# Two cached attentions on one core: V of the second in 4096 B rows, and pairs of its quads sharing P and PV

## The chip, the cores and the metric

The kernel runs on one core of a Trainium2 chip. The metric is the device time of one execution in microseconds (us), the median of the runs. A core has a matrix engine (PE, with its weight loads shown as PEld), a vector engine (DVE), an activation engine (ACT), a pool engine, and SP, which here only issues DMA transfers. 16 DMA engines move data between HBM and the on-chip SBUF. PE writes its results to PSUM, which has eight banks of 128 partitions x 2 KB; ACT and DVE read them there.

## The reference

Two independent attention blocks, A and B, whose outputs are set side by side. Both have 16 batches, 32 query tokens, a model width of 1024, 32 query heads of 128, and a cache of 1024 keys. A has 4 key/value heads (8 query heads share one), B has 32.

```python
q = (x @ wq).reshape(B, Sq, H, Dh).transpose(0, 2, 1, 3)
scores = jnp.einsum("bhqd,bhkd->bhqk", q, k) * (Dh ** -0.5)   # A: k, v repeated 8 times over heads
p = softmax(scores)
o = jnp.einsum("bhqk,bhkd->bhqd", p, v)
out = o.transpose(0, 2, 1, 3).reshape(B, Sq, H * Dh) @ wo
```

All inputs and outputs are bfloat16. B's K and V caches are 134.2 MB each; A's are 16.8 MB each, and so is the sum over all weight matrices wq (8.4 MB each for A and B) and likewise over wo.

## The kernel before

**Planning.** The program is first written down as a list of operations, each with an engine, the resources that it reads and writes, and an assumed duration (`DUR`, L35; `PACKET`, L48, for transfers). `list_schedule` (L223) then simulates the engines with these durations and fixes the order on each engine and on SP's DMA queue, and it hands out buffer slots (`Virt` objects; `SLOTS`, L90). The order is static: on the chip each engine runs its list and waits on semaphores. Operations on "any" engine go to ACT or DVE by the planner's choice. `LOOK`, `MODE_SWITCH`, `BANK_RESERVE` steer the choice.

**Quads.** Work is cut into 128 quads of A and 128 of B, interleaved. A quad is four heads-times-batches of 32 query rows each, so 128 rows of scores over 1024 keys. For B (`mk_quadB`, L720) a quad is two batches x two neighbouring heads; four quads make a group, 32 groups go through 8 blocks of 4 heads.

**The steps of a B quad** (`quadB_all`, L940):
- K comes in as two tiles of 512 KB (`st_dmaK`, L740), each holding two heads of one batch, 64 partitions per head and 16 keys per partition, so rows of 4096 B. There are 2 x `NKB_SLOTS` = 4 raw slots.
- DVE transposes each tile in 32x32 blocks of 4-byte elements into `KBt_sb` (`st_ktrB`, L782), which holds two quads.
- Scores (L827): 32 matmuls of 32 rows x 32 columns x 512 on eight tile positions of PE, planned as four operations of eight. They use all four row groups and all four column groups, because the two heads of a K tile lie on different row groups. The results go to two banks; there are two such score buffers.
- max on DVE (L837), exp with row sum on ACT (L850), which writes P in a permuted order.
- PT (`st_ptr`, L855): P, read as pairs of bf16 in 4-byte elements, is transposed by four f32 PE transposes into one PSUM bank and copied to SBUF (`st_pev`).
- V comes in as two tiles of 512 KB (`st_dmaV`, L752): 8 keys of one head per partition row, so rows of 2048 B. There are `NVB_SLOTS` = 3 quads of slots.
- PV (L892): 32 matmuls with 128 rows on four tile positions 32 columns wide, in four operations of eight.
- reciprocal, scaling by it (L908 on ACT, L909 on DVE), a transpose (L914) and a copy into `OTB_sb`, which the output projection (`oproj`) reads.

A's quads do the same with full 128x128 tiles; their K is transposed on PE (L776). The four banks of `ps_g` serve PT, PV, projections and shuffles; two of them are reserved for the projection kind "pj" while none of that kind is held.

**Q of B** is projected per group (`qprojB`), block-transposed by DVE (L625), and spread over the row groups by PE in four operations of four matmuls per group (`qprepB_sh`, L638), each evacuated to `QR`.

**Loads.** All transfers are issued by SP in the planned order; a load that has to wait for its slot holds back every later load of the queue.

Of the kernel before, what the change touches and what calls it, by code (L numbers as in the profile page):

```python
# [7 lines left out]
ALU = alu_op_type.AluOpType  # L8
# [8 lines left out]
NVB_SLOTS = 3  # L17
NKB_SLOTS = 2
# [8 lines left out]
PE_MODE = {"scoresB": 2, "Qshuf": 2, "PVB": 1}  # L27
MODE_SWITCH = 0.05
LOOK = 0.35
STEP_US = 3  # L30
STEP_NEAR = 0
ACT_FIRST = 0.3


DUR = {  # L35
    "scoresB": (0.216, 0.20), "scoresA": (0.216, 0.20), "PT_trA": (0.49, 0.22), "PT_trB": (0.49, 0.22), "PVA": (0.45, 0.22), "PVB": (0.112, 0.22),
    "OT_tr": (0.056, 0.22), "KTA_tr": (0.45, 0.22), "Qshuf": (0.107, 0.20), "qprojA": (0.432, 0.20), "qprojB": (0.432, 0.20),
    "oprojA": (0.432, 0.20), "oprojB": (0.432, 0.20), "xT_tr": (0.45, 0.22),
    "exp": (1.10, 0.12), "PT_ev@act": (0.466, 0.13), "norm@act": (0.25, 0.13), "OT_ev@act": (0.11, 0.13), "KTA_ev@act": (0.466, 0.13),
    "qA_ev@act": (0.47, 0.13), "qB_ev@act": (0.478, 0.13), "QR_ev@act": (0.252, 0.13), "acc0@act": (0.47, 0.13), "acc0@dve": (0.58, 0.12), "xT_ev@act": (0.90, 0.13),  # L40
# [3 lines left out]
    "qA_ev@dve": (0.58, 0.12), "qB_ev@dve": (0.58, 0.12), "xT_ev@dve": (0.60, 0.12), "o_fin@dve": (0.58, 0.12), "QR_ev@dve": (0.30, 0.12),  # L44
# [3 lines left out]
PACKET = {"kb_dma": (4096, 0.159), "wq_dma": (1024, 0.046)}  # L48
# [41 lines left out]
SLOTS = {"bank": 4, "P": 3, "PT": 3, "stat": 6, "O": 2}  # L90
BANK_RESERVE = {"pj": 2}
# [14 lines left out]
class Prog:  # L106
# [61 lines left out]
    def _needs_wait(self, op, d):  # L168
        if d.dma_key is not None:
            return True  # L170
        if d.eng != op.eng:
            return True
        return op.eng in self.SELF_SYNC
# [49 lines left out]
    def list_schedule(self, lat=0.05, look=LOOK):  # L223
# [39 lines left out]
        left = {v: len(l) for v, l in uses.items()}  # L263
        slot_free = {c: [0.0] * k for c, k in SLOTS.items()}
        held = {c: [None] * k for c, k in SLOTS.items()}

        def slot_time(i):

            t = 0.0
            for v in acq[i]:  # L270
                idle = [slot_free[v.cls][x] for x in range(SLOTS[v.cls]) if held[v.cls][x] is None]
                keep = sum(k for kind, k in BANK_RESERVE.items() if kind != v.kind and not any(h is not None and h.kind == kind for h in held["bank"])) if v.cls == "bank" else 0
                if len(idle) <= keep:
                    return None
                t = max(t, sorted(idle)[0])
            return t
# [34 lines left out]
        while True:  # L311
            best = None
            bkey = None
            for eng, lst in ready.items():
# [10 lines left out]
                at = {}  # L325
                for i in lst:
                    s_ = slot_time(i) if acq[i] else 0.0
                    if s_ is not None:
                        at[i] = max(ready_t[i], fe, s_) + sw(i)
# [36 lines left out]
            for u in users[best]:  # L366
                uo = ops[u]
                same_pe = (op.dma_key is None and beng == uo.eng and uo.eng == "pe")
# [62 lines left out]
def build(nc, pa, pb, out):  # L431
# [34 lines left out]
    with stack:  # L466
# [7 lines left out]
        zeros = sb("zeros", [P, P], BF)  # L474
        id32 = sb("id32", [P, P], F32)
        z32 = sb("z32", [P, P], F32)
# [4 lines left out]
        Qtok = sb("Qtok", [P, 2, NG, CW], BF)  # L481
# [7 lines left out]
        KB_sb = sb("KB_sb", [P, 2 * NKB, 16 * Dh], BF)  # L489
        KBt_sb = sb("KBt_sb", [P, 2, 2, 16 * Dh], BF)  # L490
        VB_sb = sb("VB_sb", [P, NVB, 2, 2, NCH, Dh], BF)
# [3 lines left out]
        P_sb = sb("P_sb", [P, SLOTS["P"], Sk], BF)  # L495
        PT_sb = sb("PT_sb", [P, SLOTS["PT"], NCH, P], BF)
# [11 lines left out]
        if HOOK is not None:  # L508
            print("sbuf bytes remaining per partition:", nc.sbuf_bytes_remaining() if callable(nc.sbuf_bytes_remaining) else nc.sbuf_bytes_remaining)

        pr.add("pool", lambda g: g.memset(zeros[:], 0.0), writes=["zeros"], name="c0")
        pr.add("pool", lambda g: g.affine_select(ident[:], zeros[:], [[1, P]], ALU.not_equal, 1.0, base=0, channel_multiplier=-1),
               reads=["zeros"], writes=["ident"], name="c1")
        pr.add("pool", lambda g: g.memset(z32[:], 0.0), writes=["z32"], name="c0")
        pr.add("pool", lambda g: g.affine_select(id32[:], z32[:], [[1, P]], ALU.not_equal, 1.0, base=0, channel_multiplier=-1),
               reads=["z32"], writes=["id32"], name="c1")
# [90 lines left out]
        def qprojB(m_, G):  # L607
# [4 lines left out]
            for j0 in range(0, DJ, JS):  # L612
                def e_qp(e, j0=j0):
# [5 lines left out]
                pr.add("pe", e_qp, reads=[("wq", 1, k_) for k_ in pcs] + [("xT", 1, G)], writes=[v], claims=[("Qtok", m_ % 2, G)], name="qprojB", dur=0.225 * JS,  # L619
                       rtag=dict((("wq", 1, k_), m_) for k_ in pcs))  # L620
            evac(Qtok[:, m_ % 2, G, :], lambda: bank(v)[:, 0:CW], reads=[], writes=[v, ("Qtok", m_ % 2, G)], name="qB_ev",
                 wtag={("Qtok", m_ % 2, G): m_}, mul=scale)

        def qprepB_tr(m_, G):
            pr.add("dve", lambda e: e.transpose(QBt[:, :].bitcast(F32), Qtok[:, m_ % 2, G, :].bitcast(F32)),  # L625
                   reads=[("Qtok", m_ % 2, G)], writes=["QBt"], name="QBt_tr", rtag={("Qtok", m_ % 2, G): m_}, wtag={"QBt": (m_, G)})

        def qprepB_sh(m_, G, a_list):
            gp = (m_ * NG + G) % 2
            for a in a_list:  # L630
                v = Virt("bank", "pj")

                def e_sh(e, a=a, v=v):
                    last = None
                    for rg in range(4):
                        e_ = rg // 2
                        rhs = QBt[32 * a:32 * a + 32, :].rearrange("p (hp e x) -> p e hp x", hp=2, e=2)[:, e_, :, :]
                        last = e.matmul(bank(v)[32 * rg:32 * rg + 32, 0:2 * Dh].rearrange("p (hp x) -> p hp x", hp=2),  # L638
                                        ident[32 * a:32 * a + 32, 32 * a:32 * a + 32], rhs, start=True, stop=True,
                                        tile_position=(32 * a, 32 * rg))  # L640
                    return last
                pr.add("pe", e_sh, reads=["QBt", "ident"], writes=[v], claims=[("QR", gp, a)], name="Qshuf", rtag={"QBt": (m_, G)})
                evac(QR[:, gp, a, :, :], lambda v=v: bank(v)[:, 0:2 * Dh].rearrange("p (hp x) -> p hp x", hp=2), reads=[],
                     writes=[v, ("QR", gp, a)], name="QR_ev", wtag={("QR", gp, a): (m_, G)})
# [75 lines left out]
        def mk_quadB(t):  # L720
# [7 lines left out]
            q.hp = jb % 2  # L728
            q.b0 = 4 * q.G + 2 * q.bp
            q.h0 = q.m * MS + 2 * q.hp  # L730
            q.kvslot = t % 2
            q.krslot = t % NKB
            q.vslot = t % NVB
# [3 lines left out]
            q.kid = ("B", t)  # L737
            return q

        def st_dmaK(q, t_=None):  # L740
            if q.pi == 0:
# [5 lines left out]
            else:  # L747
                sl = (2 * q.t + t_) % (2 * NKB)
                ksrc = pb["k"][q.b0 + t_, q.h0:q.h0 + 2].rearrange("hh (p s) d -> (hh p) (s d)", s=16)
                pr.add("sp", lambda e: e.dma_start(KB_sb[:, sl, :], ksrc), writes=[("KB", sl)], dma_key=f"kb{sl}", name="kb_dma", dur=2 * Sk * Dh * 2, wtag={("KB", sl): q.kid})  # L750

        def st_dmaV(q):  # L752
            if q.pi == 0:
# [5 lines left out]
            else:  # L759
                sl = q.vslot  # L760
                for t_ in range(2):
                    vsrc = pb["v"][q.b0 + t_, q.h0:q.h0 + 2].rearrange("hh (p c) d -> p hh c d", c=NCH)
                    pr.add("sp", lambda e, t_=t_, vsrc=vsrc: e.dma_start(VB_sb[:, sl, t_, :, :, :], vsrc), writes=[("VB", sl, t_)],
                           dma_key=f"vb{sl}_{t_}", name="vb_dma", dur=2 * Sk * Dh * 2, wtag={("VB", sl, t_): q.kid})
# [17 lines left out]
        def st_ktrB(q, t_):  # L782
            sl = q.kvslot
            rs = (2 * q.t + t_) % (2 * NKB)
            pr.add("dve", lambda e: e.transpose(KBt_sb[:, sl, t_, :].bitcast(F32), KB_sb[:, rs, :].bitcast(F32)),  # L785
                   reads=[("KB", rs)], writes=[("KBt", sl, t_)], name="KBt_tr", rtag={("KB", rs): q.kid}, wtag={("KBt", sl, t_): q.kid})
# [8 lines left out]
        def st_scores(q):  # L795
            q.vS = SBuf(s_rr[0] % 2)
            s_rr[0] += 1
            q.vP, q.vPT, q.vst, q.vO = Virt("P"), Virt("PT"), Virt("stat"), Virt("O")
            q.vbt, q.vbo = Virt("bank"), Virt("bank")
# [10 lines left out]
            else:  # L810
                sl = q.kvslot
                gp = (q.m * NG + q.G) % 2

                def e_s(e, fp):
                    last = None
                    if True:
                        f, pd = fp // 2, fp % 2
                        o0 = f * 64 + pd
                        for t_ in range(2):
                            a = 2 * q.bp + t_  # L820
                            for hh in range(2):
                                cg = 2 * t_ + hh
                                for g2 in range(2):
                                    rg = 2 * hh + g2
                                    lhsT = QR[32 * rg:32 * rg + 32, gp, a, q.hp, o0:o0 + 63:2]
                                    rhs = KBt_sb[32 * rg:32 * rg + 32, sl, t_, :].rearrange("p (s x) -> p s x", s=16)[:, :, o0:o0 + 63:2]
                                    last = e.matmul(ps_s[32 * cg:32 * cg + 32, vS.idx, g2, :].rearrange("p (s j) -> p s j", s=16), lhsT, rhs,  # L827
# [297 lines left out]
```

## Time and profile before

| | |
|---|---|
| runs (us) | 901.42, 905.68, 903.89; median 903.89 |
| profiled execution: span | 902.6 us |
| TensorE clock, mean granted | 0.985 |
| moved by DMA | 341.67 MB, mean 379 GB/s |
| loads of B's V | 256 of 512 KB, 8.1 us from issue to landing (median) |
| loads of B's K | 256 of 512 KB, 9.2 us |
| K transposes on DVE (L785) | 256 of 1231 ns, 311.8 us; idle before them for DMA 40.4 us |
| max (L837), exp (L850) | 256 of 1209 ns, 256 of 1119 ns |
| PT on PE (L862) | 1024 matmuls, 177.0 us |
| B's scores (L827) | 4096 matmuls, 157.2 us |
| B's PV (L892) | 4096 matmuls, 91.1 us |

Busy time of PE is the union of its matmuls, each counted with its modelled pipeline tail, so consecutive ones overlap. A group's mean is the duration of one instruction. "From issue to landing" includes the time that a transfer queues behind earlier ones. A share of the DMA engines can pass 100%, since packets of one engine overlap a little.

### The profile page before, as it was taken

Reading aid. Unit: us, or ns where it says so; the run is one execution under the profiler, and the core shown is the slowest. Engines: PE = TensorE matmul, PEld = TensorE weight load, DVE = VectorE, ACT = ScalarE, POOL = GpSimd, SP = SyncE. Lnnn points to the kernel's source line nnn. Section 1 sums busy time; section 2 is a strip of 40 time slices with the busy share of each in tenths; the row PEclk is TensorE's granted clock in tenths of the full one; section 3 lists DMA queues with packets and bytes.
Section 4 is the critical chain, followed back from the end, with each engine's and each line's share of the span. In section 5 each row is a group of like instructions: output and inputs, shape, how many; then the busy total and the mean of one; then the engine's idle time right before and its main releaser. Section 6 shows DMA issues by size and latency. Waiting matters only on the chain.

```text
span 902.6 us, 29455 instructions
## 1 busy us (share of the span) xinstructions
PE 836.3 (93%) x12864; PEld 481.8 (53%) x12864; DVE 745.3 (83%) x1057; ACT 610.8 (68%) x1384; POOL 1.1 (0%) x8
## 2 busy tenths in 40 slices
PE   6999999999899999999999998999998988999886
PEld 4365555555555555555545455555555554555453
DVE  0578897888887999689887899878979788798885
ACT  3477886677666776676776466776867666586763
POOL 0000000000000000000000000000000000000000
PEclk9999999999999999999999999999999999999999
DMA  9999999999999999999999999999999999999994
GB/s 325 383 389 393 386 385 392 390 393 383 392 387 389 393 380 388 380 386 376 387 385 391 394 369 389 388 393 370 388 387 391 392 391 367 344 393 393 393 377 170
DMA packets 153984, 341.67 MB, mean 379 GB/s; under 512 B 12544, under 2 KB 28928, under 8 KB 153856
## 3 DMA queue, kind: packets, MB, share of 16 engines
q1 hardware_dynamic: 153856, 339.79, 100.6%
q8 instruction: 102, 1.67, 0.8%
q14 instruction: 26, 0.21, 0.1%
HBM read 337.64 MB, written 2.10 MB: 376 GB/s over the span
## 4 chain that ended last, share of the span: by engine, by line
PE 48%; DMA 23%; DVE 19%; ACT 8%; SPq 1%; issue 1%; ACTq 0%; DVEq 0%
DMA KB_sb<-in_B_k_cache_dram 21%; PE ps_s L827 10%; PE ps_g L862 9%; DVE stat L837 8%; DVE KBt_sb L785 8%; PE ps_g L680 6%; ACT P_sb L850 5%; PE ps_g L892 4%; PE ps_g L598 4%; PE ps_g L884 4%; PE ps_g L616 3%; PE ps_s L806 3%; PE ps_g L776 2%; ACT PT_sb L526 1%; PE ps_g L914 1%
## 5 line engine op out<-in xcount | busy, mean ns | idle before, releaser
L785 DVE STREAM_TRANSPOSE KBt_sb<-KB_sb 128x1024 f32<-128x1024 f32 x256 | 311.8, 1231 | 42.5 <-DMA KB_sb<-in_B_k_cache_dram 40.4
L837 DVE TENSOR_REDUCE stat<-ps_s 128x1 f32<-128x1024 f32 x256 | 304.7, 1209 | 50.7 <-PE ps_s L827 34.3
L850 ACT ACTIVATE P_sb<-ps_s,stat 128x1024 bf16<-128x1024 f32 x256 | 285.8, 1119 | 51.5 <-DVE stat L837 50.0
L862 PE MATMUL ps_g<-id,P_sb 128*128 128x128 f32 x1024 | 177.0, 300 | 13.0 <-ACT P_sb L850 4.7
L862 PEld LDWEIGHTS ps_g<-id,P_sb 128*128 128x128 f32 x1024 | 150.5, 207 | 54.9 <-issue 11.1
L827 PE MATMUL ps_s<-KBt_sb,QR 32*32 32x512 bf16 x4096 | 157.2, 399 | 19.5 <-ACT P_sb L850 10.9
L526 ACT COPY PT_sb<-ps_g 128x512 f32<-128x512 f32 x234 | 134.9, 591 | 59.5 <-PE ps_g L862 58.3
L908 ACT ACTIVATE O_sb<-ps_g,stat 128x128 bf16<-128x128 f32 x199 | 71.4, 370 | 63.0 <-PE ps_g L892 32.4
L806 PE MATMUL ps_s<-KTA_sb,QT_sb 128*128 128x512 bf16 x256 | 91.5, 388 | 6.0 <-ACT P_sb L850 5.6
L827 PEld LDWEIGHTS ps_s<-KBt_sb,QR 32*32 32x32 bf16 x4096 | 49.3, 90 | 81.1 <-ACT P_sb L850 17.8
L892 PE MATMUL ps_g<-VB_sb,PT_sb 128*32 128x128 bf16 x4096 | 91.1, 224 | 1.4 <-ACT PT_sb L526 0.9
L892 PEld LDWEIGHTS ps_g<-VB_sb,PT_sb 128*32 128x32 bf16 x4096 | 60.2, 97 | 48.7 <-issue 29.2
L884 PE MATMUL ps_g<-VA_sb,PT_sb 128*128 128x128 bf16 x1024 | 78.8, 220 | 1.8 <-ACT PT_sb L526 0.7
L884 PEld LDWEIGHTS ps_g<-VA_sb,PT_sb 128*128 128x128 bf16 x1024 | 61.6, 98 | 28.2 <-issue 8.5
L616 PE MATMUL ps_g<-wq_sb,xT_sb 128*128 128x512 bf16 x256 | 71.4, 386 | 2.9 <-DMA wq_sb<-in_B_wq_dram 2.8
L680 PE MATMUL ps_g<-woB_sb,OTB_sb 128*128 128x512 bf16 x256 | 68.7, 381 | 4.4 <-ACT OTB_sb L526 1.8
L598 PE MATMUL ps_g<-xT_sb,wq_sb 128*128 128x512 bf16 x256 | 72.0, 385 | 0.3
L680 PE MATMUL ps_g<-woA_sb,OTA_sb 128*128 128x512 bf16 x256 | 63.0, 380 | 1.3 <-DVE OTA_sb L526 1.0
L914 PE MATMUL ps_g<-ident,O_sb 128*128 128x128 bf16 x256 | 51.8, 224 | 3.0 <-ACT O_sb L908 2.0
L850 ACT ACTIVATION_READ_ACCUMULATOR P_sb<-ps_s,stat 128x1 f32 x256 | 51.8, 202 | 0.0
L526 ACT COPY OTA_sb<-ps_g 128x64 f32<-128x64 f32 x114 | 24.7, 216 | 36.7 <-PE ps_g L914 36.1
L691 DVE TENSOR_TENSOR acc<-acc,ps_g 128x512 f32<-128x512 f32 x64 | 41.2, 675 | 8.1 <-PE ps_g L680 7.6
(41 smaller groups left out, 537.5 us busy)
## 6 DMA issues: line engine op xcount, KB each, us to landing
VB_sb<-in_B_v_cache_dram SPq DMA_DIRECT2D x256, 512.0 KB, 8.1
KB_sb<-in_B_k_cache_dram SPq DMA_DIRECT2D x256, 512.0 KB, 9.2
KA_sb<-in_A_k_cache_dram SPq DMA_DIRECT2D x64, 256.0 KB, 7.7
VA_sb<-in_A_v_cache_dram SPq DMA_DIRECT2D x64, 256.0 KB, 8.1
wq_sb<-in_B_wq_dram SPq DMA_DIRECT2D x32, 256.0 KB, 8.6
wq_sb<-in_A_wq_dram SPq DMA_DIRECT2D x32, 256.0 KB, 8.8
woB_sb<-in_B_wo_dram SPq DMA_DIRECT2D x32, 256.0 KB, 9.2
woA_sb<-in_A_wo_dram SPq DMA_DIRECT2D x32, 256.0 KB, 9.1
```

The source lines that it names most:

```text
L526: return e.copy(dst, src) if hasattr(e, "activation") else e.tensor_copy(dst, src)
L598: last = e.matmul(bank(v)[:, 0:tn], wq_sb[:, 0, j, hc * Dh:(hc + 1) * Dh], xT_sb[:, 0, j, t0:t0 + tn], start=(j == 0), stop=(j == DJ - 1))
L616: last = e.matmul(bank(v)[:, 0:CW], xT_sb[:, 1, j, G * P:(G + 1) * P], wq_sb[:, 1, j, :], start=(j == 0), stop=(j == DJ - 1))
L680: last = e.matmul(bank(v)[:, 0:OUTW], OT[:, gp, hh, :], wo_[:, hh, oh * OUTW:(oh + 1) * OUTW], start=(hh == 0), stop=(hh == nh - 1))
L785: pr.add("dve", lambda e: e.transpose(KBt_sb[:, sl, t_, :].bitcast(F32), KB_sb[:, rs, :].bitcast(F32)), reads=[("KB", rs)], writes=[("KBt" ...
L806: pr.add("pe", lambda e, u=u: e.matmul(ps_s[:, vS.idx, u, :], qt[:, q.b, q.hh0:q.hh0 + 4, :].rearrange("p a q -> p (a q)"), KTA_sb[:, sl, ...
L827: last = e.matmul(ps_s[32 * cg:32 * cg + 32, vS.idx, g2, :].rearrange("p (s j) -> p s j", s=16), lhsT, rhs, start=(fp == 0), stop=(fp == 3 ...
L837: pr.add("dve", lambda e: e.tensor_reduce(stat[:, vst.idx, 0:1], ps_s[:, vS.idx, :, :], AXIS.XY, ALU.max, negate=True), writes=vS.res + [v ...
L850: return e.activation(dst, src, ACTF.Exp, bias=stat[:, vst.idx, 0:1], scale=1.0, accum_out=stat[:, vst.idx, 1:2])
L862: last = e.transpose(bank(vb)[:, m * P:(m + 1) * P], p32[:, m:Sk // 2:NPK], id32[:])
L884: last = e.matmul(bank(vb)[:, 0:Dh], ptc_of(vPT, c, 0, P), VA_sb[:, kvs, c, :], start=(c == 0), stop=(c == NCH - 1))
L892: last = e.matmul(bank(vb)[32 * a:32 * a + 32, 0:Dh], ptc_of(vPT, c, 32 * a, 32 * a + 32), VB_sb[:, kvs, a // 2, a % 2, c, :], start=(c == ...
```

## The change

Two B quads now form a pair over two batches and four heads: the quad e = 0 takes the even heads (0 and 2 of the block) and e = 1 the odd ones. A K tile still holds two neighbouring heads of one batch, so each quad of a pair uses one half (64 partitions) of all four K tiles. K is transposed in place; there are 8 K slots and no `KBt_sb`. V is loaded in the same layout as K, 16 keys per partition, in rows of 4096 B and 6 slots of one tile. The exp of both quads write one P buffer of 2048 columns, interleaved so that a 128-column block of it has 64 keys of the even head and 64 of the odd one, in V's order. PT is now eight bf16 transposes per 1024 columns, and A's P is no longer permuted. PV of a pair runs as two operations of 64 matmuls, each of 64 rows x 32 columns, on eight tile positions: the upper and lower halves of the rows belong to the two quads and write to two banks. Scores are planned as one operation of 32 matmuls, which use two row groups per quad. Q's shuffle becomes two operations of eight matmuls per group, with two evacuations of a whole bank. K loads are issued after the odd quad's scores, V loads after the pair's PV. Slot counts and planner constants change; `BOOK` holds back operations that would take a bank while one that needs two banks waits for them.

```diff
-NVB_SLOTS = 3
-NKB_SLOTS = 2
+NVB_SLOTS = 6
+NQT = 5
+NKB_SLOTS = 8
...
-MODE_SWITCH = 0.05
-LOOK = 0.35
+MODE_SWITCH = 0.1
+LOOK = 0.15
...
-SLOTS = {"bank": 4, "P": 3, "PT": 3, "stat": 6, "O": 2}
-BANK_RESERVE = {"pj": 2}
+SLOTS = {"bank": 4, "P": 1, "P2": 2, "PT": 4, "stat": 8, "O": 3}
+BANK_RESERVE = {"pj": 1}
...
+                book = max((bl[i] for i in lst if pairs[i] and ready_t[i] <= fe + BOOK and slot_time(i) is None), default=None) if eng == "pe" else None
                 for i in lst:
+                    if book is not None and acq[i] and bl[i] < book and any(v.cls == "bank" for v in acq[i]):
+                        continue
...
-        KB_sb = sb("KB_sb", [P, 2 * NKB, 16 * Dh], BF)
-        KBt_sb = sb("KBt_sb", [P, 2, 2, 16 * Dh], BF)
-        VB_sb = sb("VB_sb", [P, NVB, 2, 2, NCH, Dh], BF)
+        KB_sb = sb("KB_sb", [P, NKB, 16 * Dh], BF)
+        VB_sb = sb("VB_sb", [P, NVB, 16, Dh], BF)
...
+            for name, aa in (("Qshuf", (0, 2)), ("Qshuf2", (1, 3))):
+                pr.add("pe", lambda e, aa=aa: e_sh(e, aa), reads=["QBt", "ident"], writes=vv, claims=[("QR", gp, a) for a in aa], name=name,
+                       rtag={"QBt": (m_, G)})
...
-                for t_ in range(2):
-                    vsrc = pb["v"][q.b0 + t_, q.h0:q.h0 + 2].rearrange("hh (p c) d -> p hh c d", c=NCH)
...
+                vsrc = pb["v"][qn.b0 + x // 2, qn.m * MS + 2 * (x % 2):qn.m * MS + 2 * (x % 2) + 2].rearrange("hh (p c) d -> (hh p) (c d)", c=16)
...
-            pr.add("dve", lambda e: e.transpose(KBt_sb[:, sl, t_, :].bitcast(F32), KB_sb[:, rs, :].bitcast(F32)),
+            pr.add("dve", lambda e: e.transpose(KB_sb[:, sl, :].bitcast(F32), KB_sb[:, sl, :].bitcast(F32)),
...
+                    for fp in range(4):
+                        o0 = (fp // 2) * 64 + fp % 2
+                        for cg in range(4):
+                            t_, i = cg // 2, cg % 2
+                            for g2 in range(2):
+                                r0 = 32 * (2 * q.e + g2)
+                                lhsT = QR[r0:r0 + 32, gp, 2 * q.bp + t_, i, o0:o0 + 63:2]
+                                rhs = KB_sb[r0:r0 + 32, q.ks[cg], :].rearrange("p (s x) -> p s x", s=16)[:, :, o0:o0 + 63:2]
+                                last = e.matmul(ps_s[32 * cg:32 * cg + 32, vS.idx, g2, :].rearrange("p (s j) -> p s j", s=16), lhsT, rhs,
+                                                start=(fp == 0), stop=(fp == 3), tile_position=(r0, 32 * cg))
...
+                    src = ps_s[:, vS.idx, :, :].rearrange("p g (s j) -> p g s j", s=16)
+                    dst = P2_sb[:, vP.idx, :].rearrange("p (s e g j) -> p e g s j", s=16, e=2, g=2)[:, q.e, :, :, :]
...
+        def pt_block(name, src_of, vP, vPT, vb):
             def e_pt(e):
                 last = None
+                for c in range(NCH):
+                    last = e.transpose(bankb(vb)[:, c * P:(c + 1) * P], src_of(c), ident[:])
                 return last
...
+        def st_pvB(q0, q1):
...
+            for h in range(2):
+                pt_block("PT_trB", lambda c, h=h: P2_sb[:, vP.idx, (NCH * h + c) * P:(NCH * h + c + 1) * P], vP, vPTs[h], Virt("bank"))
...
+                    for c in range(NCH):
+                        for cg in range(4):
+                            for e_ in range(2):
+                                last = e.matmul(bank(vbs[e_])[32 * cg:32 * cg + 32, 0:Dh], PT_sb[64 * e_:64 * e_ + 64, vPTs[h].idx, c, 32 * cg:32 * cg + 32],
+                                                VB_sb[64 * e_:64 * e_ + 64, q1.vs[cg], NCH * h + c, :], start=(h == 0 and c == 0), stop=(h == 1 and c == NCH - 1),
+                                                tile_position=(64 * e_, 32 * cg))
...
+        def quadB_all(q):
+            n = q.pn
+            if q.e == 0:
+                if n == 0:
+                    for x in range(4, NKB):
+                        st_dmaK(None, x)
+                for x in range(4):
+                    st_ktrB(q, x)
+            st_scores(q)
+            if q.e == 1:
+                for x in range(4 * n + NKB, min(4 * n + NKB + 4, 2 * NIT)):
+                    st_dmaK(None, x)
+            st_max(q)
+            st_exp(q)
+            if q.e == 1:
+                q0 = quadsB[q.t - 1]
+                st_pvB(q0, q)
+                for x in range(4 * n + NVB, min(4 * n + NVB + 4, 2 * NIT)):
+                    st_dmaV(None, x)
+                finish(q0)
+                finish(q)
```

## The prediction

> **What bounds the kernel now.** I read the page from the top: busy shares, the DMA rows, the chain that ended last. Then came the DMA view of short stretches, the waits of SP's queue, and the timeline of PE for the price of single operations.
>
> ```profile
> span 902.6 us, 29455 instructions
> ...
> PE 836.3 (93%) x12864; PEld 481.8 (53%) x12864; DVE 745.3 (83%) x1057; ACT 610.8 (68%) x1384; POOL 1.1 (0%) x8
> ...
> q1 hardware_dynamic: 153856, 339.79, 100.6%
> q8 instruction: 102, 1.67, 0.8%
> ...
> PE 48%; DMA 23%; DVE 19%; ACT 8%; SPq 1%; issue 1%; ACTq 0%; DVEq 0%
> ```
>
> PE at 93% is not the bound that it seems: its matmuls are counted with their pipeline tails. The packets of q1 fill 100.6% of the sixteen DMA engines' span, so the DMA has no time left. The chain names PE most because a load starts only when an engine frees its buffer, while the data queue behind other loads: a load of K lands 9.2 us and one of V 8.1 us after its issue (medians), though 512 KB are moved in about 1.3 us.
>
> How much is lost? Cutting the span into stretches of 20 us, the best ones move 393 to 396 GB/s, and the 43 stretches from 20 to 880 us average 385.5. So 860 x (1 - 385.5/393) = 16 us of DMA time are lost to moments without work for it. The rest is rate.
>
> The rate depends on the rows. The next fence holds two stretches of 4 us: in the first nearly all loads have rows of 2 KB, in the second of 4 KB (K).
>
> ```profile
> DMA packets 833, 1.56 MB, mean 390 GB/s; under 512 B 75, under 2 KB 75, under 8 KB 832
> ...
> q1 hardware_dynamic: 832, 1.55, 104.7%
> ...
> DMA packets 467, 1.63 MB, mean 407 GB/s; under 512 B 50, under 2 KB 50, under 8 KB 467
> ...
> q1 hardware_dynamic: 467, 1.63, 103.8%
> ```
>
> Without the small packets (semaphores) these are 1.56 MB / 758 = 2058 B and 1.63 MB / 417 = 3909 B a packet. Both stretches are full (share over 103%), yet one moves 390 and the other 407 GB/s. Neighbouring cuts give 388 (from 385 to 389 us) and 410 (404.2 to 407.6), so I use 389 and 408.
>
> **The change, part by part.**
>
> V in 4 KB rows. All 256 loads of V, 134.2 MB, go from 2 KB to 4 KB packets: 134.2/0.389 = 345.0 us become 134.2/0.408 = 328.9. That is **-16 us** on the full resource. The bounds are 0 (V's source strides cancel it) and -17.7 (410 GB/s). The semaphore packets do not change, as there are 256 loads of V before and after, each still 512 KB.
>
> The Trainium skill speaks against this part: its page "DMA: Bandwidth & Descriptors", section Specifications, gives 512 B as the smallest transfer that reaches the line rate, so rows of 2 KB would already be there. By it this term would be 0. The two stretches above, 390 against 407 GB/s, do not agree with it.
>
> Instruction fetch. PT goes from 4 transposes of f32 per quad to 8 of bf16 (1024 to 2048 matmuls), and PV from 32 matmuls of 128 rows per quad to 64 of 64 rows (4096 to 8192). With a weight load each that is 2 x (1024 + 4096) = 10240 more instructions at 64 B (1.88 MB of q8 and q14 for 29455 instructions): 0.66 MB. q8's 1.67 MB took 0.8% of 902.6 = 7.2 us, so **+2.8 us** (bounds 0, if it only fills DMA gaps, and 2.8).
>
> PE. This timeline has the prices (start, duration, operation, count):
>
> ```profile
> 404.64 1.13 PE L827 MATMUL ps_s<-KBt_sb,QR 32*32 32x512 bf16 x32
> ...
> 46.66 0.63 PE L862 MATMUL ps_g<-id,P_sb 128*128 128x128 f32 x4
> 47.22 0.43 PE L827 MATMUL ps_s<-KBt_sb,QR 32*32 32x512 bf16 x8
> ...
> 48.58 0.63 PE L892 MATMUL ps_g<-VB_sb,PT_sb 128*32 128x128 bf16 x32
> 49.14 0.43 PE L827 MATMUL ps_s<-KBt_sb,QR 32*32 32x512 bf16 x8
> 49.50 0.62 PE L884 MATMUL ps_g<-VA_sb,PT_sb 128*128 128x128 bf16 x8
> ```
>
> From start to next start the four f32 transposes hold PE 0.56 us (46.66 to 47.22). Eight matmuls of 128x128 bf16 hold it 0.46 (49.50 to 49.96, the next start): 256 x -0.10 = -26 us. PV's 32 matmuls on four tiles hold 0.56 (48.58 to 49.14), one round of four per 0.06. On eight tiles a quad's 64 are eight rounds again. If a round of eight runs as one of four, +0; if PE takes the same 14 ns per matmul, 64 x 0.0144 + 0.1 = 1.02, or +0.46 x 128 = +59. The scores' eight tiles in 0.43 (L827 x8: one matmul lasts 0.40, so eight start within 0.03) are nearest, since those are also eight tiles; I take +15. Scores keep eight tiles per round, with two row groups where there were four. The bound above is rounds of four, 8 x 0.23 against 4 x 0.23, +0.9 x 128 = +118. The bound below is the gain from no longer being cut in four, 1.44 to 1.07 us (x8 holds 0.36, x32 1.07), at 57 fewer pieces (185 in the timeline now, 128 then) x 0.12 = -7; I take -7. The nearest row for one row group feeding several tiles is the shuffle (L638), whose four matmuls of 256 columns on one row group end in 0.29 us, no longer than one alone (0.28). Q's shuffle: 128 operations at 0.22 become 64 of about 0.25, -12 us. PE's sum is **-30 us** by my values, between -45 and +139 (-26 + 59 + 118 - 12). All of it lies beside the DMA, so I put it at 0 in the sum. Without that cover the chain would feel PE's part of it, 48%: -14 us by my values, +67 at the worst end, which I count under (b) below.
>
> ACT and DVE. The evacuation of Q's shuffle goes from 128 of about 0.39 us to 64 of about 0.6, -12 us. Exp, max (1.21 us), PT's evacuation (0.59) and the transposes of K (1.23, now in place) keep shape and count. All of it is hidden: DVE is busy 83% of the time. 0 in the sum, at most -12.
>
> Buffers and queue order. K held two quads raw and two transposed; now eight tiles hold two pairs. After the odd quad's scores SP issues four K loads, after the pair's PV four V loads. Behind SP's waits stand the loads of A's K and V and of the weights. Timing by pairs: 902.6/64 = 14.1 us a pair. A burst of four K loads lands 9.2 to 9.2 + 3 x 1.3 = 13.1 us after issue, and its four transposes end by 14.4, against some 20 us until the next-but-one pair's even scores. Of the V burst, the first two tiles are for the next pair, landing at 8.1 and 9.4 us against 14 until its PV. So both have 4 us or more to spare: 0, bounded by -16 (all lost DMA time comes back) and by the rival below.
>
> Start and end. The first loads keep their order, weights and x ahead of K and V. The end stays about 14 us behind the last loads (DMA share 0.07 from 890 to 902.6), because V's last two tiles come only after the last PV but one: 0, between -3 and +5 (a V load took at least 4.3 us to land).
>
> Sum: 902.6 - 16 + 2.8 = 889.4 us of span. The median of the runs, 903.89, stands 1.3 above the profiled span, so **890.7 us**, which is 1.5% less.
>
> **Rivals.**
> (a) V's rows change nothing: 903.9 + 2.8 = 906.7. For it speaks only that V's 2 KB packets may share a limit with K's that a short stretch hides; against it, the two full stretches.
> This is also what the Trainium skill's 512 B (same page and section) would give.
> (b) Slower: the pair's PV holds too much. A V slot is freed by fours, only after both halves of PV, and in that time the pair holds two PV banks and two PT banks of the four, so A's PV and the projections wait, and with them the scores that free K. Place: SP's wait before V. The present waits there are already the largest:
>
> ```profile
> SPq L763 <- PE ps_g L892: 136.7, 69, 7.4
> SPq L750 <- DVE KBt_sb L785: 115.2, 77, 5.2
> ```
>
> It decides once the queue runs dry more than (16 - 2.8)/64 = 0.21 us longer per pair than now. At 0.7 us per pair the price is 64 x 0.7 = 45 us: 890.7 + 45 - 16 (of the present loss, which it swallows) = 920. Against it: nobody waits for V in the trace, and 4 us are to spare.
> (c) Better: K's deeper slots and the lighter PE also fill the DMA's gaps, 890.7 - 14 = 877. For it: DVE still waits 40.4 us for K, and the gap stretches (319 GB/s from 318 to 322 us) follow late buffer releases; against it, the coarser bursts.
>
> **How the numbers follow.** Forecast 0.56 (its own range 881 to 899), (a) 0.10, (b) 0.22, (c) 0.12. This measurement cannot tell less than about 0.5% (899.4 to 908.4) from no change. Faster is the forecast without its slow edge plus (c), 0.66; same is (a) and that edge, 0.12; slower is (b), 0.22. The range leaves out about half of (b), above 917, and the far end of (c), below 871.
>
> **What would show it.** Right: under 121,500 packets on q1 for the same bytes, best stretches of 400 GB/s or more, q1's share still near 100%, PE's groups for PT and the shuffle smaller, no wait of PE on V. PV on eight tiles is right if 64 matmuls end in 0.7 us, wrong at 1.1; the scores are right at 1.1 us for 32. Rival (a) shows as full stretches at 390 GB/s; (b) as a q1 share well under 100% with longer waits of SP before V; (c) as an average close to the best stretches. The prediction falls if PE waits for V or for K, or if the DMA is no longer full.

## The result and the profile after

The changed kernel takes 1039.86 us (median of 4 runs, 1029.7 to 1049.9) against 904.75 us before; the ratio is 1.146, with a 95% interval from 1.140 to 1.152. The ratio leaves out the run of 1049.9 us, which fell in a slower state. It is 15% slower, where 1.5% faster was forecast, and far outside the range.

The head of the page after, its DMA rows and the shares of the chain that ended last:

```profile
span 1036.8 us, 39415 instructions
...
PE 840.4 (81%) x17829; PEld 507.8 (49%) x17984; DVE 736.0 (71%) x1014; ACT 608.5 (59%) x1363; POOL 0.7 (0%) x6
...
PEclk9989999889887988999988989989899999888987
...
q1 hardware_dynamic: 121088, 339.79, 88.1%
q8 instruction: 141, 2.31, 0.8%
...
PE 63%; issue 15%; DVE 12%; ACT 7%; DMA 2%; SPq 1%
```

No engine has noticeably more work than before: PE is busy 840 us (836 before), DVE 736 (745), ACT 609 (611). The DMA is no longer full, 88.1% after 100.6%, and the chain hardly waits for it, 2% after 23%. What is new is "issue" with 15% of the span, 155 us, where it had 1%: time in which an engine waits for nothing that the profile shows. 155 us is more than the whole loss of 134 us. PE's granted clock fell as well, from 0.985 to 0.904 on average.

The waits, longest in total first (engine, operation, what it waited for: us in total, times, longest), show which engine that is. After:

```profile
PEld ps_g L903 <- issue: 96.5, 68, 4.7
...
PE ps_g L903 <- issue: 74.9, 32, 4.6
...
PEld ps_s L839 <- issue: 44.0, 62, 3.6
```

The row of PV's weight loads before, the largest of its kind:

```profile
PEld ps_g L892 <- issue: 29.2, 72, 0.5
```

Before, "issue" was short pauses: 72 at PV, of 0.5 us at most, and none above 0.8 us in any row of the weight loads. Now PE stands still for up to 4.7 us with nothing to wait for. PE's timeline shows one such place (start, duration, operation, count, idle time before):

```profile
509.49 1.13 PE L839 MATMUL ps_s<-KB_sb,QR 32*32 32x512 bf16 x32
510.56 1.30 PE L903 MATMUL ps_g<-VB_sb,PT_sb 64*32 64x128 bf16 x128
511.79 0.62 PE L869 MATMUL ps_g<-ident,P_sb 128*128 128x128 bf16 x8
512.32 0.23 PE L925 MATMUL ps_g<-ident,O_sb 128*128 128x128 bf16 x1
513.22 0.42 PE L839 MATMUL ps_s<-KB_sb,QR 32*32 32x512 bf16 x7 [0.67 <-ACT P_sb L862]
515.77 1.07 PE L839 MATMUL ps_s<-KB_sb,QR 32*32 32x512 bf16 x25 [2.13 <-issue]
...
517.50 3.35 PE L688 MATMUL ps_g<-woB_sb,OTB_sb 128*128 128x512 bf16 x8
```

The scores of one quad are a single operation of 32 matmuls, and they stop after 7 of them: their waits were over, since seven had run. A bare lack of instructions remains. Just before, PV sent 128 matmuls with 128 weight loads through PE in 1.30 us. And 2 us behind the stop the eight matmuls of the projection take 3.35 us, 0.42 each; in the kernel before four of them took 1.03 us, 0.26 each:

```profile
417.55 1.03 PE L680 MATMUL ps_g<-woB_sb,OTB_sb 128*128 128x512 bf16 x4
```

The same place after the change by stretches, with the granted clock behind the busy times:

```profile
505.00:513.00 8.00, 7.29 (x234) 4.96 (x228) 6.97 (x14) 6.72 (x14) 0.00 (x0) 1.00 1.05 407
513.00:516.00 3.00, 0.65 (x15) 0.25 (x23) 1.84 (x2) 1.01 (x5) 0.00 (x0) 1.00 1.03 397
516.00:518.00 2.00, 2.00 (x36) 1.17 (x21) 1.12 (x1) 0.47 (x2) 0.00 (x0) 0.76 1.04 418
518.00:520.50 2.50, 2.50 (x8) 0.87 (x7) 2.50 (x4) 1.32 (x3) 0.00 (x0) 0.51 1.03 415
```

The columns are PE, PEld, DVE, ACT, POOL, clock, DMA share, GB/s. After the pause the clock is down to 0.51 for 2.5 us, so the work behind the pause is slow as well. The last two columns show the rows of 4 KB at work: full stretches (share 1.03 to 1.05) at 397 to 418 GB/s.

**Where the pauses lie.** I took all idle times of 0.9 us or more in the timeline of the weight loads that end on "issue", and counted PE's instructions (matmuls and weight loads) from one to the next:

```
at us    idle us  PE instructions since the last one
497.87   1.65      508
515.77   2.45      748
530.02   3.60      508
548.11   4.71      506
563.52   1.04      508
581.83   0.98      750
596.00   2.94      504
610.97   3.35      506
```

There are 52 such pauses, 142.7 us in sum; before there were none. Nearly all lie at a multiple of about 254 PE instructions from the one before. The queue q8 counts the same way: the change added 10,240 PE instructions and 39 packets, 263 to a packet, and a packet carries 16 KB (2.31 MB / 141). So PE gets its program in blocks of about 256.

That a pause is a block that has not come can be seen in the packets of q8 one by one, which the trace holds with their times. Of the 52 pauses, 51 end 1.2 to 1.6 us after a packet of q8 has ended, though such a packet comes only every 7 us or so; 36 of these packets started only after PE had stopped. At each pause the number of instructions that PE had run (twice its weight loads) is 186 plus 253.7 for every packet landed so far, to within 22. The pause that ends at 515.77 us began at 513.32, and its packet lies in the window from 513.5 to 514.5 us:

```profile
q8 instruction: 1, 0.02, 5.9%
```

5.9% of sixteen engines over 1 us is 0.94 us. The median packet took 0.95 us, against 1.09 us in the kernel before, so the transfer of a block is not slow: it starts too late.

The Trainium skill has this on its page "Runtime: NRT & Kernel Launch", section "Instruction fetch mechanics": blocks of 16 KiB, 256 instructions, the next fetched while the current one runs. The trace agrees with the block. The same section calls the cost of crossing a block's edge mostly hidden, and here 52 of 141 edges cost 2.7 us each.

### The profile page after: what moved, and what is told of

Same layout as the page of the kernel before. It is cut to its first block, busy times and chain, and to the rows that moved or that the text cites. A ratio compares the mean times of both kernels' runs of the same rounds, so it can differ in the third digit from the quotient of the medians.

```text
span 1036.8 us, 39415 instructions
## 1 busy us (share of the span) xinstructions
PE 840.4 (81%) x17829; PEld 507.8 (49%) x17984; DVE 736.0 (71%) x1014; ACT 608.5 (59%) x1363; POOL 0.7 (0%) x6
## 2 busy tenths in 40 slices
DMA packets 121254, 342.30 MB, mean 330 GB/s; under 512 B 12544, under 2 KB 28928, under 8 KB 121088
## 3 DMA queue, kind: packets, MB, share of 16 engines
q1 hardware_dynamic: 121088, 339.79, 88.1%
q8 instruction: 141, 2.31, 0.8%
## 4 chain that ended last, share of the span: by engine, by line
PE 63%; issue 15%; DVE 12%; ACT 7%; DMA 2%; SPq 1%
PE ps_s L839 13%; PE ps_g L688 11%; PE ps_g L869 10%; PE ps_g L903 6%; DVE stat L849 6%; PE ps_g L884 5%; PE ps_g L601 5%; PE ps_g L619 4%; ACT P_sb L862 4%; DVE KB_sb L795 4%; PE ps_s L822 4%; PE ps_g L925 2%; PE ps_g L787 2%; ACT PT_sb L529 1%; DMA VB_sb<-in_B_v_cache_dram 1%
## 5 line engine op out<-in xcount | busy, mean ns | idle before, releaser
L795 DVE STREAM_TRANSPOSE KB_sb<-KB_sb 128x1024 f32<-128x1024 f32 x256 | 308.3, 1223 | 6.3 <-DMA KB_sb<-in_B_k_cache_dram 6.0
L839 PE MATMUL ps_s<-KB_sb,QR 32*32 32x512 bf16 x4096 | 162.4, 421 | 34.5 <-issue 25.3
L869 PE MATMUL ps_g<-ident,P_sb 128*128 128x128 bf16 x2048 | 159.4, 229 | 18.1 <-issue 7.1
L869 PEld LDWEIGHTS ps_g<-ident,P_sb 128*128 128x128 bf16 x2048 | 134.7, 103 | 63.1 <-issue 15.2
L903 PE MATMUL ps_g<-VB_sb,PT_sb 64*32 64x128 bf16 x8192 | 92.7, 227 | 77.0 <-issue 74.9
L903 PEld LDWEIGHTS ps_g<-VB_sb,PT_sb 64*32 64x32 bf16 x8192 | 77.8, 91 | 105.1 <-issue 96.5
L884 PE MATMUL ps_g<-VA_sb,PT_sb 128*128 128x128 bf16 x1024 | 88.1, 236 | 14.6 <-issue 13.3
L839 PEld LDWEIGHTS ps_s<-KB_sb,QR 32*32 32x32 bf16 x4096 | 52.5, 93 | 96.5 <-issue 44.0
L822 PE MATMUL ps_s<-KTA_sb,QT_sb 128*128 128x512 bf16 x179 | 66.1, 409 | 12.4 <-issue 6.3
L529 ACT COPY OTB_sb<-ps_g 128x64 f32<-128x64 f32 x113 | 20.2, 216 | 66.0 <-PE ps_g L925 65.6
```

What stands on the lines that cost most here:

```text
L529: return e.copy(dst, src) if hasattr(e, "activation") else e.tensor_copy(dst, src)
L795: pr.add("dve", lambda e: e.transpose(KB_sb[:, sl, :].bitcast(F32), KB_sb[:, sl, :].bitcast(F32)), writes=[("KB", sl)], name="KBt_tr", rta ...
L822: pr.add("pe", lambda e, u=u: e.matmul(ps_s[:, vS.idx, u, :], qt[:, q.b, q.hh0:q.hh0 + 4, :].rearrange("p a q -> p (a q)"), KTA_sb[:, sl, ...
L869: last = e.transpose(bankb(vb)[:, c * P:(c + 1) * P], src_of(c), ident[:])
L884: last = e.matmul(bank(vb)[:, 0:Dh], PT_sb[:, vPT.idx, c, :], VA_sb[:, kvs, c, :], start=(c == 0), stop=(c == NCH - 1))
L903: last = e.matmul(bank(vbs[e_])[32 * cg:32 * cg + 32, 0:Dh], PT_sb[64 * e_:64 * e_ + 64, vPTs[h].idx, c, 32 * cg:32 * cg + 32], VB_sb[64 * ...
```

## The experiments

Theory **F**: PE's instructions are the bound. The change raised them from 25,728 to 35,968 and put 256 of them into 1.3 us; the next blocks come too late. The rival **R** is the prediction's rival (b): pairs, buffers freed by fours and the bank shortage hold things up.

**e1: more instructions, nothing else of the change.**

```diff
-  last = e.matmul(bank(vb)[32 * a:32 * a + 32, 0:Dh], ..., VB_sb[:, kvs, a // 2, a % 2, c, :],
+  last = e.matmul(bank(vb)[32 * a:32 * a + 32, x0:x0 + 64], ..., VB_sb[:, kvs, a // 2, a % 2, c, x0:x0 + 64],
...
+  for x0, c0 in ((0, 0), (0, 4), (64, 0), (64, 4)):
```

> Kernel before; each of PV's 4096 matmuls of 128 columns is cut into two of 64, with a weight load each: 8192 more PE instructions, same buffers, loads and results. Theory F (PE's instructions arrive in blocks of 256 and the block is late when PE runs through one faster than the next comes): stalls of PE on issue of 1 us and more appear, 930 to 1040 us. Theory R (pairs, freed by fours, and the bank shortage cost the time): nothing of that is in here, 900 to 912 us.

Measured: 952.96 us, ratio 1.055 (1.051 to 1.059). The kernel before, given 8192 more instructions on PE, loses 49 us; 24 long pauses of 42.6 us in sum appear, 8 of them at PV:

```profile
PEld ps_g L892 <- issue: 45.7, 85, 2.9
```

F as expected. R has no part in this kernel. Not all of the 49 us need be pauses: PE's busy time rose as well, from 836.3 to 857.1 us.

**e2: the change with half of PV's instructions.**

```diff
-                    for c in range(NCH):
+                    for c in (0, 2, 4, NCH - 1):
```

> Changed kernel; B's PV leaves out every second key chunk: 4096 matmuls and 8192 PE instructions less, pairs, banks, slots, loads and their order as in the changed kernel. F: long issue stalls of PE almost gone, 880 to 915 us. R: PV's own time was only 93 us and mostly beside other work, so above 1010 us.

Measured: 876.77 us, ratio 0.971 (0.968 to 0.974). All of the pair scheme is in it, and it is 163 us faster than the change. The page's rows for instructions and the chain:

```profile
q8 instruction: 110, 1.80, 0.7%
...
PE 41%; DVE 28%; DMA 17%; ACT 10%; issue 3%; SPq 1%; DVEq 0%
```

SP's wait before V, in the view of the waits of e2:

```profile
SPq L774 <- PE ps_g L903: 124.7, 41, 7.1
```

PE's busy time fell by only 840.4 - 770.8 = 70 us, and 9 long pauses of 15.6 us are left. R can hardly be the cause: banks, slots by fours and late V loads are all still there, though PV holds its banks for a shorter time. In the changed kernel the same wait of SP before V was 227.6 us in 55 times; it grows with PE's pauses, with the same pairs and slots in both kernels.

**e3: the rows of V alone.**

```diff
-  vsrc = pb["v"][...].rearrange("hh (p c) d -> p hh c d", c=NCH)
+  vsrc = pb["v"][...].rearrange("hh (p c) d -> (hh p) (c d)", c=2 * NCH)
```

> Kernel before; V is loaded in rows of 4096 B into the same slots, so PV multiplies V's rows in another order. No instruction more. If the row size has the worth that the prediction gave it: -16 us, 884 to 893 us. If the row size is worth nothing (rival a): 901 to 908 us.

Measured: 892.7 us, ratio 0.989 (0.985 to 0.992), 11 us faster than before. The row size is worth something, and rival (a) is out. It is worth less than the 16 us of the sum; by the chain, which hardly waits for the DMA any more (3% after 23%), PE takes over once the DMA is quicker.

```profile
PE 66%; DVE 18%; ACT 10%; DMA 3%; issue 1%; SPq 1%; DVEq 0%; ACTq 0%
```

**e4: PV in two bursts.** The second half of PT reads a token that the first half of PV writes.

```diff
+ pt_block("PT_trB", ..., ["PVhalf"])
- pr.add("pe", e_pv, reads=[vPTs[h]] + vt, writes=vbs, ...
+ pr.add("pe", e_pv, reads=[vPTs[h]] + vt, writes=vbs + ["PVhalf"], ...
```

> Changed kernel; the second half of a pair's PT is made to follow the first half of its PV, so that PV runs as two bursts of 64 matmuls with other PE work between, not as one of 128. Same instruction count. F, if the burst is what outruns the block: fewer or shorter issue stalls, 920 to 1000 us. F, if the mean rate of instructions is: about 1030 us. R: the PV banks are held longer, so not faster, 1030 us or more.

Measured: 984.91 us, ratio 1.091 (1.086 to 1.095): 55 us less than the change with exactly its instructions. Still 52 long pauses, but of 102.5 us. The burst matters beside the count. The two banks of a pair's PV are in use for longer than in the change, 4.4 us against 1.7 us in median from its first weight load to its last, and still the kernel is faster. By R it would not have been faster, so with all instructions in place R fails again.

**e5: is the block late because the DMA is full?**

```diff
+                if vt >= NVB:
+                    pr.vtag[("VB", sl)] = ("B", n, x)
+                    return
```

> Changed kernel; of B's V only the first six tiles are loaded, PV goes on reading them: 250 loads of 512 KB left out, all instructions of PE as in the changed kernel. Theory F1 (a block of instructions comes late because its transfer queues behind the data): with 40% less data the long issue stalls shrink to under 60 us in sum, below 930 us. F2 (the fetch is as slow by itself): 110 to 150 us of such stalls stay, 980 us or more.

Measured: 947.95 us, ratio 1.051 (1.048 to 1.054), 38 long pauses of 84.1 us, with q1 at 61.7% of the engines' span. That lies between both expectations. Less data traffic takes away some 40% of the pauses; more than half of them stay with the DMA idle a third of the time. All 38 end 1.2 to 1.7 us after a packet of q8, and the median packet took 0.95 us as in the change, so here too the block started late and was not slow.

**e6: eight blocks fewer.** P transposed as f32 pairs.

```diff
-                    last = e.transpose(bankb(vb)[:, c * P:(c + 1) * P], src_of(c), ident[:])
+                    last = e.transpose(bank(vb)[:, m * P:(m + 1) * P], src_of(m), id32[:])
```

> Changed kernel; P is transposed as pairs of bf16 in f32, as in the kernel before: 1024 transposes for 2048, 2048 PE instructions less of 35968, eight blocks of 141. F: fewer blocks, so a little faster, 990 to 1025 us. R: transposes are not on the path of buffers and banks, 1030 us or more.

Measured: 1018.41 us, ratio 1.128 (1.126 to 1.129), 45 pauses of 123.2 us. A little faster, as F has it.

**e7 and e8: an order that knows the blocks.** In the planner an operation of PE starts no earlier than its block is there:

```diff
+        def fetch(i):
+            return fetched[(n_pe[0] + PE_INSTR[ops[i].name] - 1) // BLOCK]
...
+                        fetched[b_ + 1] = max(st, fetched[b_]) + BLOCK_US
```

> As e6, and the planner knows that a block of 256 PE instructions can be entered only 5.5 us after the one before it was entered, so that it spreads the dense operations; LOOK 0.2, MODE_SWITCH 0.05, PV's duration 0.6. F: long issue stalls under 40 us, 870 to 920 us, so perhaps faster than the kernel before. R: 1010 us or more.

> Changed kernel with all its 35968 PE instructions; only the order is new: the planner knows the 5.5 us per block (MODE_SWITCH 0.05, ACT_FIRST 0.1, PV's duration 0.6). F: long issue stalls under 70 us, 890 to 950 us. R, or a fetch that is too slow on average: above 1000 us.

Measured: e7 1023.92 us, ratio 1.134 (1.128 to 1.139), 45 pauses of 114.3 us; e8 1016.18 us, ratio 1.126 (1.123 to 1.129), 41 pauses of 100.4 us. Both miss what F expected of them. The packets of q8 show that this says little against F. Over the whole run they came 3.3 to 14.4 us apart in e8 (the middle 80% of them 4.0 to 10.6 us), where the change had 3.3 to 15.6 us (3.6 to 11.1 us): the spacing that was planned hardly arose on the chip. It was most even from 480 to 620 us, 4.5 to 8.25 us in e8 where the change had 3.5 to 12.75, and there e8 has six pauses of 10.5 us in sum, the change nine of 23.8 us. That fits F. Whether 5.5 us is the right price of a block, and how late a block may be asked for, stays open.

**e9: the change's instruction count in the kernel before.** e1, and P in eight bf16 transposes.

```diff
-                    last = e.transpose(bank(vb)[:, m * P:(m + 1) * P], p32[:, m:Sk // 2:NPK], id32[:])
+                    last = e.transpose(bankb(vb)[:, c * P:(c + 1) * P], P_sb[:, vP.idx, c:Sk:NCH], ident[:])
```

> Kernel before with PV cut as in e1 and P transposed in eight bf16 transposes per quad: 35968 PE instructions, as many as the changed kernel, but quad by quad with the buffers and loads of before. F by count alone: as slow as the changed kernel, 1010 to 1050 us. F by count and burst (a pair's PV is 256 instructions in 1.3 us, a quad's here 128 in 0.6): 960 to 1005 us. R: 900 to 912 us.

Measured: 978.11 us, ratio 1.078 (1.072 to 1.083), 30 pauses of 60.7 us. Without pairs, with the old buffers and loads, the added instructions cost 75 us of the change's 135. By count alone it would have been as slow as the change, so the count is not all. That the rest goes with its burst is not shown by this run; e4, with the burst cut in two, gains 55 us.

**e10: halfway.**

```diff
-                    for c in range(NCH):
+                    for c in (0, 1, 2, 4, 5, NCH - 1):
```

> Changed kernel; B's PV leaves out two of eight key chunks: 4096 PE instructions less, halfway between the changed kernel and e2. F: the time lies between 877 and 1040, 930 to 985 us, and the long issue stalls between 16 and 143 us. R: above 1010 us.

Measured: 945.91 us, ratio 1.046 (1.040 to 1.052), 37 pauses of 84.9 us: between e2 and the change in time and in pauses.

**e11: both repairs.** The edits of e4 and e6 together.

> Changed kernel with both repairs, PV in two bursts as in e4 and P transposed in f32 as in e6; nothing left out. F: the gains of e4 (55 us) and e6 (20 us) add, 950 to 985 us; still above the kernel before. R: 1030 us or more.

Measured: 960.88 us, ratio 1.065 (1.062 to 1.069), 35 pauses of 73.5 us. The gains add (55 + 21 expected, 79 found), and it is the best complete version of the pair scheme that I found. It does not reach the kernel before.

All kernels in one table. The last column takes the chain's share of issue off the span.

| | PE instructions | q8 blocks | long pauses, us | issue in the chain | span, us | span less issue |
|---|---|---|---|---|---|---|
| before | 25,728 | 102 | 0 | 1% | 902.6 | 894 |
| e3 | 25,728 | 102 | 1 | 1% | 892.2 | 883 |
| e2 | 27,776 | 110 | 16 | 3% | 875.7 | 849 |
| e10 | 31,872 | 126 | 85 | 10% | 944.5 | 850 |
| e1 | 33,920 | 133 | 43 | 5% | 957.0 | 909 |
| e11 | 33,920 | 133 | 73 | 8% | 960.9 | 884 |
| e6 | 33,920 | 133 | 123 | 12% | 1021.7 | 899 |
| e7 | 33,920 | 134 | 114 | 12% | 1015.6 | 894 |
| e9 | 35,968 | 142 | 61 | 9% | 980.5 | 892 |
| e5 | 35,968 | 141 | 84 | 11% | 945.9 | 842 |
| e4 | 35,968 | 141 | 102 | 10% | 979.1 | 881 |
| e8 | 35,968 | 141 | 100 | 11% | 1019.1 | 907 |
| after | 35,968 | 141 | 143 | 15% | 1036.8 | 881 |

The spans differ by 161 us, the last column by 67 (by 60 without e5, which loads less), with no order by instruction count left in it. That ties the loss to issue, as closely as shares in whole per cent (5 us each way) can. e2, e5 and e10 also leave out work or loads.

## Why the prediction was wrong

**The step that failed** is "Instruction fetch", priced at +2.8 us. The count of 10,240 more instructions and the 0.66 MB were right, and q8 shows 39 packets more. But I priced only what these packets take from the data on the DMA, not what PE loses while it waits for one. By the chain its cost was some 146 us ("issue": 15% of 1036.8 less 1% of 902.6). With it fell the sentence that all of PE's terms lie beside the DMA: PE's work indeed did not grow, its supply ran dry.

**PE's operations** came out as priced or better. 128 matmuls of PV on eight tiles end in 1.30 us, 0.65 per half, and hold PE 1.23 us to the next start (510.56 to 511.79), 0.61 per quad against 0.56 before: some +7 us, between the lower bound of 0 and the +15 that I took. The scores with two row groups stay at 1.13 us. Q's shuffle fell from 41.0 to 20.9 us. PT's group fell from 177.0 to 159.4, less than the 26 us of the sum, though with PE's clock at 0.904. This speed is part of the trouble: the faster the tiles run, the sooner a block is used up.

**V's rows** were right in kind. q1 needs 121,088 packets, full stretches move 397 to 418 GB/s, and e3 gains 11 us, where the sum had 16 (bounds 0 and 17.7). The doubt that the Trainium skill's 512 B raised ("DMA: Bandwidth & Descriptors", Specifications) does not hold here. In the changed kernel this gain is hidden, since the DMA waits.

**Rival (b)** had the right sign and the wrong mechanism. The sign to look for, a q1 share well under 100% with longer waits of SP before V, came exactly so, yet e2 has the same pairs, banks and slots at 877 us, and e4 holds the banks longer and gains 55. The sign could not tell the two causes apart. **Rival (c)**, the better case at 877 us, is where e2 ends up, but by chance: e2 leaves out some 42 us of PE's time in PV (92.7 to 50.3) and still has 15.6 us of long pauses. What the scheme would take with its instructions in time, no run shows.

**Unsettled**: how much of the loss is the halved clock after a pause; no run here had pauses without it. Also why a block's transfer starts as late as it does, why the planned spacing of e7 and e8 hardly arose, and why e8, with pauses of 100 us, is 31 us slower than e4 with 102.

## What to carry to other kernels

Count the instructions of each engine, and how many fall into the densest microseconds, before small tiles replace large ones: here 256 PE instructions in 1.3 us and 141 blocks in place of 102 cost 15%, though no engine got more work. In a profile, pauses that end on "issue", longer than in a version without the trouble (0.8 us at most here) and at multiples of some 254 instructions, point to a late block of program; the packets of the instruction queue confirm it if the pauses end a fixed time after them (1.2 to 1.6 us here). When an engine is slow, the waits of everyone else grow too, so take the suspected cause away alone before believing them.

## What was not expected of the hardware

PE stood still for a block of its program for up to 4.7 us in the change, and for up to 3.5 us in e5, where the DMA is not full (84 us of pauses at 61.7%). The block's own packet took only 0.95 us (median) in both.

PE's granted clock was 0.51 from 518 to 520.5 us, behind a pause. The mean over the run is lower in kernels with pauses, though not strictly in their order: 0.985 with none, 0.980 with 43 us (e1), 0.961 with 16 us (e2), 0.947 with 102 us (e4), 0.904 with 143 us, 0.899 with 123 us (e6). The Trainium skill's page "TensorE: Matmul & The Clock Gate", section "Why this matters for your kernels", advises no idle gaps of PE above about 3 us for this reason. At 513 to 516 us two gaps of 0.67 and 2.13 us, seven matmuls apart, came before the slow stretch. Nor is a long pause needed: the kernel before was at 0.50 from 373 to 376.3 us, with gaps of 0.82 and 0.26 us as the longest in the 5 us before.
